# Block-sparse attention and a feed-forward net in one planned kernel: weight splits due later, late attention steps due later, one last eviction on VectorE

## The chip, the cores and the metric

The kernel runs on one NeuronCore of a Trainium2 chip. The metric is the device time of one execution in microseconds. Three executions of the kernel before took 785.02, 786.54 and 787.48 us; the median is 786.54 us.

## The reference

The inputs are `q`, `k` and `v` of shape (4, 8, 768, 64), three sampled key blocks for each of 24 query blocks, and two weight matrices `w_in` (512 x 2048) and `w_out` (2048 x 512), the weights and the samples in 64 bits.

```python
scores = scale * np.matmul(q, k.transpose(0, 1, 3, 2))
# a block of 32 queries sees: its own block and its neighbours, blocks 0 and 23, three sampled blocks;
# query blocks 0 and 23 see all keys
attn = softmax(np.where(mask, scores, -1e9))
x = (attn @ v).transpose(0, 2, 1, 3).reshape(3072, 512)
h = x @ w_in
out = (h - np.tanh(h)) @ w_out
```

## The kernel before

**Feed-forward units.** The 3072 tokens are cut into six chunks of 512 (`CHUNKS`, four query blocks of all four batches each), the 2048 hidden features into 16 tiles of 128. One pair of chunk and tile is a unit; there are 96 of them, numbered by `UNITS`. The first two chunks are worked off in halves: units 0 to 7 are the first half of chunk 0, 8 to 23 are chunk 1, 24 to 31 the second half of chunk 0, 32 to 47 chunk 2, and so on to 95. A unit has twelve matmuls of the first layer (`first`, four groups of three, as each operand is kept as a high and a low part), a bend of the hidden values by nine elementwise operations (`bent`), and twelve matmuls of the second layer (`second`, four groups of three, one for each 128 tokens), which come two and a half units later.

**Attention steps.** Attention for later chunks is worked off in steps beside the units. A step has 32 score products into banks 6 and 7 (`scores`), row maxima on VectorE (`most`), exponentials on ScalarE (`exps`), eight transposes on TensorE back into banks 6 and 7 (`turn`), two copies out of them (`copy`), 64 value products into bank 4 or 5 (`accum`), a normalisation on VectorE (`norm`), and a high and a low part written into the chunk's operand on ScalarE and GpSimd (`put`). Query blocks 0 and 23 see all keys; their steps come in threes (`EDGES`), have a single copy as their `norm`, and are joined afterwards by small VectorE operations (`weigh`, `join`). Ten early steps run before and around unit 0. `SLOTS` gives each later step its unit. In the tables for chunks 3, 4 and 5 (`m` of 3, 4, 5) a chunk of 16 units has eleven slots, at offsets 0, 1, 2, 4, 5, 7, 8, 10, 11, 13 and 14; ten of them are used in the last one. So 32 steps belong to these chunks.

**Order.** Nothing is scheduled freely. Each piece of work is put on a list with a due time in units (`at`), the list is sorted by due time, ties by the order of entry, and every engine keeps exactly that order (`InOrder`), SyncE's queue of transfers included. Due times of unit u: the four groups of `first` at u + 0, 0.125, 0.25, 0.375; the four groups of `second` for unit u - 2 at u + 0.5, 0.625, 0.75, 0.875; the nine operations of the bend by `STEPS`, of which `w`, `hs`, `t`, `qq`, `mk` and `gh` are ScalarE's, `p1`, `p2`, `p3` and `cp` VectorE's, `gl` GpSimd's and `th` GpSimd's up to unit 31 and VectorE's from 32 on. `cp`, due at u + 1.49, is the last that reads the hidden values' bank, 4 or 5 in turn. A step in slot s has its scores at s + 0.55, its row maxima at s + 0.63, its exponentials at s + 0.75 and 0.85, its transposes at s + 1.21 (where the next slot is the next unit) or s + 1.55, its copies 0.05 and 0.06 later, and its value products at 0.52 past the start of the next slot, 0.1 before the normalisation. The value products at u + 0.52 go to the bank of unit u - 1, so they need that unit's `cp` as well as the copies.

**Weights.** The 64-bit weights are turned into 32-bit ones on the chip, 32 tiles of 128 x 1024 words. `convert` is three VectorE operations, the first two through a spare PSUM bank. `split` writes the high part on ScalarE and the low part on GpSimd, `save` writes both to memory by SyncE for later units (`get`). Four tiles are converted before unit 0, the other 28 at the times in `CONVA` (twelve in units 0 to 7) and `CONVB` (every 0.93 units from 8.2 on). `split` is due 0.03 units after the third operation of its conversion, `save` 0.4 after it.

**The end.** `store` evicts the four accumulators of a chunk, j = 0 and 2 on ScalarE and j = 1 and 3 on VectorE, and sends each out in four transfers; for the last chunk those of j = 0 and 2 are issued by ScalarE's queue, those of j = 1 and 3 by SyncE's.

Of the kernel before, what the change touches and what calls it, by code (L numbers as in the profile page):

```python
# [11 lines left out]
F32 = mybir.dt.float32  # L12
# [5 lines left out]
ALU = mybir.AluOpType  # L18
# [4 lines left out]
P = 128  # L23
# [3 lines left out]
DM, DFF = 512, 2048  # L27
# [5 lines left out]
NU = NTOK // P // CT * NFT  # L33

LEAD, T0, RATE = 10, 10.25, 0.62
QUICK, TURN = 0.66, 1.0
NQ = 4
KEPT = 3
VW = H * (D + 1) // 2
# [27 lines left out]
class InOrder:  # L67


    class Engine:  # L70
        def __init__(self, tc, engine):
            self.tc, self.engine = tc, engine
# [44 lines left out]
class Unit:  # L117
# [27 lines left out]
    def at(self, half, j):  # L145

        return (half, self.b) if self.b else (self.f, (NB - 1) * half)


class Attention:  # L150
    def __init__(self, tc, k, q, v, samp, rows, ffn, ident, banks, att, sm, f2, rv, at):
        self.tc, self.nc = tc, InOrder(tc)
        self.k, self.q, self.v, self.ffn, self.ident, self.banks = k, q, v, ffn, ident, banks
        self.sm, self.f2, self.att, self.rv = sm, f2, att, rv
        self.ks = att.tile([P, 2, H, S], F32, name="ks")
        self.vws, self.krs, self.loans = {}, {}, {}
        ffn.lent = self.lent
        self.kx, self.vx = (att.tile([1, 66], I32, name=f"{n}x") for n in "kv")
        self.held = {}
        self.vals, self.qs, self.ve = {}, {}, {}  # L160
        self.ms, self.nbs, self.ps, self.pts, self.nbe, self.es, self.wts = ({} for _ in range(7))
        self.kept = [ffn.spare.bitcast(F32)[:, 256 * i : 256 * i + 256] for i in range(3)]

        units = []
        last = {}

        def add(c, time, **kw):
            u = Unit(len(units), c, time, **kw)
            u.i, u.before = c, last.get(c)
            if u.n < LEAD - 2:  # L170
                u.i, u.before = u.n % 2, units[u.n - 2] if u.n > 1 else None
            elif u.n < LEAD:
                u.before = units[u.n - 2]
            if u.b:
                last[c] = u
            units.append(u)

        for c in range(2):
            for b in CHUNKS[0]:
                add(c, 0, b=b)  # L180
        for c in range(2):
            add(c, 0, b=CHUNKS[1][0])
        for m, blocks in list(enumerate(CHUNKS))[1:]:
            steps = [(c, dict(b=b)) for b in blocks if 0 < b < NB - 1 for c in range(2)]
            edges = [(g // 2, dict(f=g % 2, k=k)) for g in EDGES.get(m, ()) for k in range(3)]
            steps += edges
            for i, (c, kw) in enumerate(steps[2 * (m == 1) :]):
                slots = SLOTS[m - 1]
                following = slots[i + 1] if i + 1 < len(slots) else 16 * m if m > 2 else slots[i] + 1
                add(c, slots[i] + 0.55, prod=following + 0.52, **kw)  # L190
        lead = lambda x: (x - T0) * RATE
        for u in units[:2]:
            at(lead(-9.05), self.load_q, u)
        for bt in range(2):
            at(lead(-9), self.load_k, 0, bt)
        at(lead(-9.1), self.load_samples, samp, rows)
        for bt in range(2):
            at(lead(-8.9), self.load_k, 1, bt)
        for u in units:
            t, n = u.t, u.n  # L200
            if u.b:
                if n > 1:
                    at(max(t["s"] - 2.0, units[n - NQ].t["s"] + 0.01) if n >= NQ else lead(-8.95 + 0.01 * n), self.load_q, u)
                at(max(t["s"] - 1.2, u.before.t["s"] + 0.01 if u.before else lead(-3)), self.gather_k, u)
                at(max(t["s"] - 2.0, u.before.t["pv"] + 0.01) if u.before else lead(-3 + 0.1 * n), self.gather_v, u)
            else:
                if u.k == 0:
                    at(units[n - 1].t["s"] + 0.02, self.load_q, u)
                at(units[n - 2].t["pv"] + 0.02, self.load_ve, u)
            at(t["s"], self.scores, u)  # L210
            at(t["m"], self.most, u)
            at(t["e1"], self.exps, u, 1)
            at(t["e0"], self.exps, u, 0)
            at(t["turn"], self.turn, u)
            at(t["c1"], self.copy, u, 1)
            at(t["c0"], self.copy, u, 0)
            at(t["pv"], self.accum, u)
            at(t["norm"], self.norm, u)
            if u.b:
                for x in "hl":  # L220
                    at(t["norm"] + (0.1 if x == "h" else 0.15), self.put, u, x)
            elif u.k == 2:
                at(t["e0"] + 0.12, self.weigh, u)
                end = 2 * u.c + u.f in EDGES[len(CHUNKS) - 1]
                quiet = iter([t["norm"] + 0.1 + 0.08 * j for j in range(6)] if end else self.quiet(units[u.n + 1 :], t["norm"]))
                for k in range(3):
                    for s in range(1 + k):
                        at(next(quiet), self.join, u, k, s)
                for i in range(2):
                    for x in "hl":  # L230
                        at(t["norm"] + 0.65 + 0.2 * i if end else LATE + 0.5 * (2 * u.c + u.f) + 0.25 * i, self.put, u, x, i)
# [250 lines left out]
class FFN:  # L482
# [134 lines left out]
    def store(self, n, j):  # L617
        nc = self.nc
        end = n == len(CHUNKS) - 1
        if n == 0:  # L620
            ob = self.work.pop(("sum", j))
            nc.vector.scalar_tensor_tensor(out=ob, in0=self.acc[j], scalar=-1.0, in1=ob, op0=ALU.mult, op1=ALU.add)
        elif j % 2:
            if n == 1:
                ob = self.spare.bitcast(F32)[:, DM * (j // 2) : DM * (j // 2) + DM]
            else:
                ob = self.f2.tile([P, DM], F32, tag="wcvt", name=f"ob{n}_{j}")
            nc.vector.tensor_scalar(out=ob, in0=self.acc[j], scalar1=-1.0, scalar2=None, op0=ALU.mult)
        else:
            ob = self.rv.tile([P, 1040], F32, tag="rv", name=f"ob{n}_{j}")[:, 0:DM]  # L630
            nc.scalar.activation(out=ob, in_=self.acc[j], func=AF.Copy, scale=-1.0)
        eng = nc.scalar if end and j % 2 == 0 else nc.sync
        for bt in range(B):
            r0 = S * bt + BLK * CHUNKS[n][j]
            eng.dma_start(out=self.out[r0 : r0 + BLK, :], in_=ob[BLK * bt : BLK * bt + BLK])

    def plan(self, at):
        t, done = lambda x: (x - T0) * RATE, []
# [3 lines left out]
        slots = [(t(4.5 + 1.6 * k), 0.3 * RATE, None) for k in range(4)] + [(x, 0.09, banks[b]) for x, b in zip(CONVA, CONVAB)]  # L642
        slots += [(CONVB[0] + CONVB[1] * k, 0.12, banks[6 + k % 2]) for k in range(2 * HALF)]
        free = []
        for k, ((m, ft), (t0, dt, tmp)) in enumerate(zip(halves[0] + halves[1], slots)):
            at(max(t0 - 1.8, free[k - 3] if k > 2 else -99), self.load, m, ft, k)
            for x in range(3):
                at(t0 + dt * x, self.convert, m, ft, x, tmp)
            end = t0 + 2 * dt
            at(end + 0.03 + 0.35 * (k == len(slots) - 1), self.split, m, ft)  # L650
            if ft >= KEPT:
                at(end + 0.4, self.save, m, ft)
            free.append(end + 0.01)
            done.append((m, UNITS.index((ft // HALF, ft))))
        self.ends = [e for e in ENDS if e != 2 * HALF]
        for u in range(NU):
            n, ft = UNITS[u]
# [10 lines left out]
            end = u == NU - 1  # L668
# [52 lines left out]
```

## Time and profile before

| what | value |
|---|---|
| median of three runs | 786.54 us |
| the profiled execution | 785.86 us, of which its span is 784.1 us |
| TensorE matmul busy | 728.9 us, 93% |
| VectorE busy | 549.9 us, 70% |
| ScalarE busy | 479.2 us, 61% |
| GpSimd busy | 337.2 us, 43% |
| mean granted TensorE clock | 0.98 |

The profile calls TensorE's matmuls PE and its weight loads PEld, VectorE DVE, ScalarE ACT, GpSimd POOL and SyncE SP; a trailing q is an engine's own queue of transfers. Names on the left of an arrow are what an instruction writes, on the right what it reads: `ps` is any PSUM bank, `vw,pt` and `ve,pt` the value products, `kr,q` and `ks,q` the scores, `ident,p` the transposes, `x,wi` (also `wri`, `li`) the first layer and `wo,gh` and `wo,gl` (also `wro`, `lo`) the second. `cvti` and `cvto` are converted tiles, `wi` and `wo` what a split writes. All instructions have one line, L78, that of a helper that records the order. "Busy" time of matmuls is modelled at its end, so start times are the firmer numbers.

### The profile page before, as it was taken

What the parts mean: (1) busy time and instruction counts of PE and PEld (TensorE: products, weight loads), DVE (VectorE), ACT (ScalarE), POOL (GpSimd) and SP (SyncE); (2) the same over time, 40 slices, a digit from 0 to 9 for tenths busy, and PEclk for the clock granted to TensorE, in tenths of its full rate; (3) what the DMA queues carried; (4) which work ended last, traced back from release to release, by engine and by line L of the source; (5) the groups of instructions that cost most, each with busy time, mean ns of one, the idle gap of its engine ahead of it and who ended that gap; (6) DMA issues with size and microseconds to landing.
All of it is one profiled execution on the core that took longest, in us unless ns stands there. A gap on an engine that the chain in (4) does not pass through costs nothing.

```text
span 784.1 us, 20699 instructions
## 1 busy us (share of the span) xinstructions
PE 728.9 (93%) x8128; PEld 564.7 (72%) x8128; DVE 549.9 (70%) x970; ACT 479.2 (61%) x1021; POOL 337.2 (43%) x406
## 2 busy tenths in 40 slices
PE   1777887999999999999999999999999998999996
PEld 0555555878777777777777777777877776788884
DVE  4566777779875765777676678676777675875653
ACT  1576756577767766565665666665666555554553
POOL 3685764667687646244322434321432211221211
PEclk9899999999999999999999999999999999999998
DMA  8887674489685686275746166565157364246542
GB/s 347 268 268 239 201 224 161 164 320 363 228 262 171 193 275 205 79 233 175 280 149 205 37 200 230 185 228 184 69 158 265 127 217 163 82 135 219 187 158 80
DMA packets 54260, 155.49 MB, mean 198 GB/s; under 512 B 9107, under 2 KB 15764, under 8 KB 53652
## 3 DMA queue, kind: packets, MB, share of 16 engines
q1 hardware_dynamic: 53780, 153.65, 58.6%
q8 instruction: 64, 1.05, 0.5%
q10 hardware_dynamic: 384, 0.52, 0.2%
q14 instruction: 32, 0.26, 0.1%
HBM read 133.17 MB, written 20.97 MB: 197 GB/s over the span
## 4 chain that ended last, share of the span: by engine, by line
PE 71%; DVE 7%; ACT 3%; issue 2%; POOL 1%; DMA 0%; DVEq 0%; POOLq 0%
PE ps L78 71%; DVE ps L78 3%; DVE t L78 1%; POOL gl L78 1%; DVE m L78 0%; ACT p L78 0%; ACT t L78 0%; DVE e L78 0%; ACT hs L78 0%; ACT wo L78 0%; ACT u L78 0%; DVE ob L78 0%; DVE cvti L78 0%; DVE cvto L78 0%; ACT gh L78 0%
## 5 line engine op out<-in xcount | busy, mean ns | idle before, releaser
L78 PE MATMUL ps<-x,wi 128*128 128x512 f32 x888 | 221.2, 393 | 0.0
L78 POOL TENSOR_TENSOR gl<-t,gh 128x512 fp32r<-128x512 f32 x96 | 124.3, 1295 | 215.3 <-ACT gh L78 69.5
L78 PE MATMUL ps<-wo,gh 128*128 128x512 f32 x592 | 192.2, 407 | 0.0
L78 PEld LDWEIGHTS ps<-x,wi 128*128 128x128 f32 x888 | 164.9, 188 | 35.5
L78 PEld LDWEIGHTS ps<-wo,gh 128*128 128x128 f32 x592 | 108.6, 190 | 36.9 <-issue 15.0
L78 ACT ACTIVATE u<-ps 128x512 f32<-128x512 f32 x96 | 57.3, 597 | 108.2 <-PE ps L78 108.2
L78 PE MATMUL ps<-wo,gl 128*128 128x512 f32 x296 | 117.6, 399 | 0.7 <-POOL gl L78 0.7
L78 POOL TENSOR_TENSOR x<-xt,x 128x256 fp32r<-128x256 f32 (+1 forms) x48 | 34.3, 715 | 161.8 <-ACT x L78 158.3
L78 POOL COPY kr<-ks 128x256 f32 (+2 forms) x188 | 98.5, 617 | 11.9 <-DMA ks<-k 11.7
L78 DVE TENSOR_REDUCE m<-ps 128x2 f32<-128x512 f32 x112 | 70.9, 673 | 19.1 <-PE ps L78 17.2
L78 DVE COPY_PREDICATED t<-mk,ps 128x512 f32<-128x512 int32 x96 | 71.8, 748 | 10.1 <-DVE ps L78 0.9
L78 DVE TENSOR_TENSOR ps<-ps,u 128x512 f32<-128x512 f32 x96 | 66.5, 692 | 13.7 <-ACT t L78 13.7
L78 ACT ACTIVATE p<-ps,nb 128x256 f32<-128x256 f32 x176 | 73.8, 471 | 2.9
L78 DVE SCALAR_TENSOR_TENSOR ps<-qq,ps 128x512 f32<-128x512 f32 x96 | 66.4, 692 | 12.9 <-ACT qq L78 8.6
L78 PEld LDWEIGHTS ps<-vw,pt 128*32 128x32 f32 x2816 | 44.4, 113 | 38.6 <-DVE t L78 10.1
L78 PE MATMUL ps<-vw,pt 128*32 128x65 f32 x2816 | 52.5, 227 | 20.4 <-DMA vw<-v 9.3
L78 ACT ACTIVATE qq<-u,bias 128x512 f32<-128x512 f32 x96 | 69.3, 722 | 0.0
L78 ACT ACTIVATE mk<-u,bias 128x512 f32<-128x512 f32 x96 | 69.1, 720 | 0.0
L78 DVE SCALAR_TENSOR_TENSOR ps<-u,ps 128x512 f32<-128x512 f32 x96 | 66.6, 693 | 2.5
L78 DVE TENSOR_TENSOR t<-t,ps 128x512 f32<-128x512 f32 x64 | 43.5, 680 | 35.2 <-ACT t L78 35.1
L78 PE MATMUL ps<-ident,p 128*128 128x128 f32 x448 | 62.4, 283 | 5.6 <-ACT p L78 4.2
L78 PEld LDWEIGHTS ps<-wo,gl 128*128 128x128 f32 x296 | 56.1, 189 | 15.4 <-POOL gl L78 1.9
(98 smaller groups left out, 980.2 us busy)
## 6 DMA issues: line engine op xcount, KB each, us to landing
wi<-w2i SPq DMA_DIRECT2D x65, 512.0 KB, 4.7
wo<-w2o SPq DMA_DIRECT2D x65, 512.0 KB, 3.7
vw<-v SPq DMA_DIRECT2D x186, 130.0 KB, 2.9
q<-q SPq DMA_DIRECT2D x52, 128.0 KB, 4.3
ve<-v SPq DMA_DIRECT2D x24, 260.0 KB, 4.0
ks<-k SPq DMA_DIRECT2D x4, 1536.0 KB, 8.4
rawo<-w SPq DMA_DIRECT2D x12, 512.0 KB, 4.3
rawi<-w SPq DMA_DIRECT2D x10, 512.0 KB, 4.7
```

What stands on the lines that cost most here:

```text
L78: r = f(*args, **kw)
```

## The change

Four due times and one engine change:

- Steps of chunks 3, 4 and 5 have every due time 0.08 units later. Their scores are due at s + 0.63, their value products at 0.60 past the next slot.
- `split` of the 28 tiles converted from unit 0 on is due 0.3 units after the conversion's third operation in place of 0.03; the last tile's stays at 0.38. `save` is due 0.65 after it in place of 0.4.
- For early steps 0 to 7, `put` is due 0.02 and 0.03 after `norm` in place of 0.1 and 0.15.
- In `store` of the last chunk, j = 2 is evicted by VectorE. Its transfers stay on ScalarE's queue.

```diff
-QUICK, TURN = 0.66, 1.0
+QUICK, TURN, SHIFT = 0.66, 1.0, 0.08
...
-                add(c, slots[i] + 0.55, prod=following + 0.52, **kw)
+                add(c, slots[i] + 0.55 + SHIFT * (m > 2), prod=following + 0.52 + SHIFT * (m > 2), **kw)
...
-                    at(t["norm"] + (0.1 if x == "h" else 0.15), self.put, u, x)
+                    at(t["norm"] + (0.1 if x == "h" else 0.15) * (0.2 if n < LEAD - 2 else 1), self.put, u, x)
...
+        elif end and j:
+            ob = self.rv.tile([P, 1040], F32, tag="rv", name=f"ob{n}_{j}")[:, 0:DM]
+            nc.vector.tensor_scalar(out=ob, in0=self.acc[j], scalar1=-1.0, scalar2=None, op0=ALU.mult)
         else:
...
-            at(end + 0.03 + 0.35 * (k == len(slots) - 1), self.split, m, ft)
+            at(end + (0.03 if t0 < 0 else 0.38 if k == len(slots) - 1 else 0.3), self.split, m, ft)
             if ft >= KEPT:
-                at(end + 0.4, self.save, m, ft)
+                at(end + 0.65, self.save, m, ft)
```

## Rows read from the trace of the kernel before

**Rows 1.** Busy time by stretch: us, then busy us (instructions) of each engine, clock, DMA

```profile
core 0: us, PE busy (x) PEld busy (x) DVE busy (x) ACT busy (x) POOL busy (x), PEclk, DMA share, GB/s
62.00:142.00 80.00, 64.80 (x912) 47.24 (x911) 57.58 (x110) 54.00 (x120) 48.24 (x57) 0.91 0.63 201
142.00:680.00 538.00, 531.97 (x5905) 415.39 (x5904) 393.57 (x684) 343.33 (x729) 227.47 (x268) 1.00 0.58 196
```

**Rows 2.** TensorE's waits, whole span: total us, times, longest us

```profile
PE ps L78 <- ACT wo L78: 7.3, 4, 2.1
...
PE ps L78 <- DVE t L78: 4.3, 5, 2.2
```

**Rows 3.** Timeline of all engines, unit 5: start, duration, what, [idle before, releaser]

```profile
125.74 0.72 DVE L78 COPY_PREDICATED t<-mk,ps 128x512 f32<-128x512 int32 x1
125.85 0.63 ACT L78 ACTIVATE wo<-cvto 128x512 fp32r<-128x512 f32 x1 [2.28 <-DVE cvto L78]
...
126.56 0.26 PE L78 MATMUL ps<-vw,pt 128*32 128x65 f32 x4 [1.64 <-ACT wo L78]
```

**Rows 4.** Timeline of TensorE, one group of the second layer ahead of transposes

```profile
406.37 0.63 PE L78 MATMUL ps<-wo,gh 128*128 128x512 f32 x2
...
407.07 1.03 PE L78 MATMUL ps<-ident,p 128*128 128x128 f32 x8
```

**Rows 5.** Timeline of TensorE in unit 65, a step's products between second-layer groups

```profile
568.05 0.63 PE L78 MATMUL ps<-wo,gh 128*128 128x512 f32 x2
...
568.84 1.11 PE L78 MATMUL ps<-vw,pt 128*32 128x65 f32 x64
569.88 1.09 PE L78 MATMUL ps<-kr,q 64*32 64x256 f32 x32
570.91 0.73 PE L78 MATMUL ps<-wo,gh 128*128 128x512 f32 x2
...
573.11 1.08 PE L78 MATMUL ps<-x,wri 128*128 128x512 f32 x4
```

**Rows 6.** Timeline of TensorE in unit 78, value products with no scores behind

```profile
673.52 1.11 PE L78 MATMUL ps<-ve,pt 128*32 128x65 f32 x64
674.57 0.73 PE L78 MATMUL ps<-wo,gh 128*128 128x512 f32 x2
...
676.77 1.08 PE L78 MATMUL ps<-x,wi 128*128 128x512 f32 x4
```

**Rows 7.** Timeline of VectorE around the products of rows 5

```profile
566.50 0.69 DVE L78 COPY pt<-ps 128x512 f32<-128x512 f32 x1 [0.88 <-PE ps L78]
...
567.90 0.74 DVE L78 COPY_PREDICATED t<-mk,ps 128x512 f32<-128x512 int32 x1
...
571.26 1.25 DVE L78 TENSOR_REDUCE m<-ps 128x2 f32<-128x512 f32 x2
```

**Rows 8.** Timeline of VectorE in unit 74: the row maxima

```profile
640.25 1.29 DVE L78 TENSOR_REDUCE m<-ps 128x2 f32<-128x512 f32 x2 [0.64 <-PE ps L78]
```

**Rows 9.** Timeline of VectorE in unit 78: the end of unit 77's bend

```profile
672.72 0.75 DVE L78 COPY_PREDICATED t<-mk,ps 128x512 f32<-128x512 int32 x1
```

**Rows 10.** Timeline of all engines, unit 1

```profile
77.21 0.63 ACT L78 ACTIVATE wro<-cvto 128x512 fp32r<-128x512 f32 x1 [1.51 <-DVE cvto L78]
...
79.47 0.66 PE L78 MATMUL ps<-ident,p 128*128 128x128 f32 x4 [2.45 <-ACT p L78]
...
80.89 0.73 DVE L78 COPY_PREDICATED t<-mk,ps 128x512 f32<-128x512 int32 x1
...
82.44 0.66 PE L78 MATMUL ps<-vw,pt 128*32 128x65 f32 x16
```

**Rows 11.** Timeline of all engines, unit 0: last early step and first layer

```profile
63.20 0.45 DVE L78 STREAM_TRANSPOSE xt<-x 128x256 f32<-128x256 f32 x1
...
66.28 0.57 PE L78 MATMUL ps<-x,wri 128*128 128x512 f32 x1 [2.08 <-ACT x L78]
```

**Rows 12.** Timeline of the end: transfers of the last chunk by two queues

```profile
777.38 3.63 SPq L78 DMA_DIRECT2D out<-ob  x8
...
779.61 1.85 ACTq L78 DMA_DIRECT2D out<-ob  x4
```

## The prediction

> **What bounds the kernel now.** I read the busy times by stretch first, then TensorE's waits, then the timelines where a due time moves past another. From 142 to 680 us TensorE's matmuls are busy 532.0 of 538 us at the full clock [rows 1]: there TensorE's own order is the time, and nothing done elsewhere can give back more than 6 us. From 62 to 142 us it is busy 64.8 of 80 us, with a mean granted clock of 0.91, so some 14 us of these ran at the lower level, 1.2 GHz [rows 1]. Here the other engines set the time.
>
> The list of waits names the splits of output weights as the largest releaser in this stretch: four waits, 7.3 us [rows 2], and one part of the change moves exactly these. I don't take the name at its word. In one of the four, the predicated copy that ends a unit's bend runs 125.74 to 126.46 and the split 125.85 to 126.48; the value products start at 126.56 [rows 3]. Both end within 0.02 us, and by the code the products read nothing that the split writes, but they overwrite the bank that the predicated copy has just read. Both follow the same conversion. So the true releaser is VectorE, whose list in these units (two conversions, the bend, the row maxima, the normalisation) is the loop; ScalarE's split is beside it.
>
> **The shift by 0.08, on TensorE.** The second-layer groups of a unit are due at 0.5, 0.625, 0.75 and 0.875. Before, value products (0.52) and scores (0.55) lay together between the first two. After, value products (0.60) still lie there, but scores (0.63) come behind the second group by 0.005. The order group, values, scores, three groups becomes group, values, group, scores, two groups: one return to the second layer and one departure more. What these cost: a group of three with transposes behind takes 407.07 - 406.37 = 0.70 us [rows 4]. With value products behind it takes 568.84 - 568.05 = 0.79 [rows 5]. A departure costs 0.09. Three groups behind scores take 573.11 - 570.91 = 2.20 [rows 5], behind value products alone 676.77 - 674.57 = 2.20 [rows 6], against 3 x 0.70 = 2.10. A return costs 0.10, from either kind. Going straight from values to scores adds nothing that is saved now: the 64 products take 1.04 us with scores behind (569.88 - 568.84) and 1.05 with a group behind (674.57 - 673.52) [rows 5, 6].
>
> So 0.19 us for each slot where values and scores meet: 32 slots less the first, which has no values of an earlier step that moves with it, is 31. 31 x 0.19 = 5.9 us. No idle time covers it: all such stretches show TensorE with no gap but five waits of 4.3 us in total [rows 2]. The transposes (1.21 to 1.29, or 1.55 to 1.63) pass one group as well, but stand between two groups of the same layer before and after: no switch more.
>
> What the departure from values to scores would cost is in no row for scores; taken as for values. The bounds: nothing, if the scores' weights load under the group in between (0.10 x 31 = 3.1 us in all), and twice that of values (0.28 x 31 = 8.7).
>
> A rule of the Trainium skill speaks against this term. TensorE: Matmul & The Clock Gate, section "Step-by-step: what each phase is for", says that TensorE pulls weight loads ahead of matmuls in flight, so that the next tile's weights load while this one runs. By that, a change of shape would cost nothing and the term would be 0. The trace does not agree: 0.09 and 0.10 us stand at each such switch.
>
> **The shift, on VectorE.** Scores end 0.89 us later after the value products (0.70 + 0.10 + 0.09), and the row maxima wait for them. In a usual step this fits. In unit 65 the copy out of the transposes waited 0.88 us with the bend's third product queued behind it, and the predicated copy ended at 568.64, ready for the value products at 568.84 [rows 5, 7]. After, the copy (due 0.34) stands behind that product (0.27), which fills the gap: copy at 566.50 + 0.89 = 567.39, 0.7 for it and 0.74 for the predicated copy makes 568.83, against 568.84 + 0.19 = 569.03 on TensorE. The row maxima of steps with the full normalisation start at 571.26, 0.35 us behind the scores' end at 570.91 [rows 5, 7]; they lose less than 0.89.
>
> Two places have no such gap. In unit 74 five joins follow the maxima, VectorE is full to the predicated copy, and the value products already wait 2.2 us [rows 2]. The maxima there wait for the scores alone (0.64 idle, [rows 8]), so all 0.89 goes through: 0.89 - 0.19 = 0.7 more. In unit 77 the weights of the joins lie in the chain; its predicated copy ends 673.47 and the products start 673.52 [rows 6, 9]: again 0.7. Where a chunk's accumulators are evicted (due in units 33, 49 and 65) an eviction or a join moves into the time in which VectorE waits for the value products, which about pays for the later maxima. Of the 2.1 us of other waits [rows 2] 0.2 may be taken up. Together 5.9 + 0.7 + 0.7 - 0.2 = 7.1 us more. ScalarE's order (the high part of the bend ahead of the exponentials) and GpSimd's (low parts and key gathers 0.08 later) have room in these units.
>
> **The splits.** In units 3 to 6 VectorE is the loop, and ScalarE's list between the row maxima and the two copies stays as long: the input split that stood ahead of the copies goes behind them, while the output split, now due at 0.77, comes in between the two exponentials. I take nothing; the bounds are 7.3 us back, if the profile's releaser were the true one, and 2 us lost, if the exponentials' delay reaches the transposes. In unit 1 ScalarE is the bound: it idles 1.51 us for a conversion ahead of a split, with half a step's exponentials queued behind, and the second transposes wait 2.45 us [rows 10]. After, the split is due at 1.23, behind them, and the transposes can go up to 1.51 + 0.63 = 2.1 us earlier. But the value products then wait for the predicated copy, which ends at 81.62 where they start at 82.44 [rows 10]: 0.8 us. With a little for the other early units: 1.0. In units 8 to 31 TensorE is full and the splits are off its path; 0.5 of the 6 us of idle time up to 680 us [rows 1], as ScalarE's first squares of a unit no longer stand behind a split. GpSimd's low parts and the saves on SyncE come later too: the value gathers for a step, due at 0.53, now go out ahead of an input tile's save (0.69 in place of 0.44), and no get of a saved tile is nearer than five units.
>
> **The early puts.** The last early step's tile is transposed at 63.65, but ScalarE writes its part only after two sets of exponentials and copies, and the first layer waits 2.08 us for it [rows 11]. After, the put stands ahead of them. But for all eight early steps ScalarE then stops for the normalisation, with the next steps' exponentials and copies behind it, and the early steps follow each other more strictly. I take 0.5 us gained, between 2.1 gained and 2 lost.
>
> **The end.** ScalarE's eviction of the third quarter stood behind its own first four transfers; its last transfer was issued at 779.61 + 1.85 = 781.46, SyncE's at 777.38 + 3.63 = 781.01 [rows 12]. After, VectorE has the tile ready early, ScalarE's queue ends before SyncE's, and SyncE's is last: 0.45 gained. SyncE's own order is unchanged.
>
> **Sum.** 7.1 - 1.0 - 0.5 - 0.5 - 0.45 = 4.65 us. The profiled execution took 785.86 us (span 784.1), so 790.5; it lies 0.7 below the median of 786.54, which gives 791.2. I say 791.0.
>
> **Rivals.** *The profile's releaser is right* (14%): the four waits of 7.3 us are the splits' own and go. 791.0 - 7.3 = 783.7, and 784 to 786 if VectorE holds the products for part of it. Not slower. For it: the name in the list. Against: the code and the common end. It decides once more than 4.65 us come back.
>
> *The switch hides* (9%): the scores' order costs TensorE nothing, and only VectorE's 1.2 us stay. 791.0 - 5.9 = 785.1. This is where the skill's rule above would lead. Against: every switch in rows 5 and 6.
>
> *The later maxima hold every close pair* (10%): 17 pairs of steps lie in adjacent units; 13 beside those named. If swapping the copy and the product returns nothing, each loses up to 0.5: 791.0 + 6.5 = 797.5. Against: the 0.88 us gap.
>
> *The early part gets longer* (9%): ScalarE stopped by puts, and key gathers on GpSimd behind the later low parts, so that scores in units 4 and 5 come late. 2 us each: 795.
>
> *My forecast* (58%): own range 788 to 794, as the lower clock in the early units may fall on other places; a stretch of it costs up to half its length.
>
> **The numbers.** What a measurement of this kernel can tell from no change is about 0.3%, 2.4 us: 784.2 to 788.9. The forecast falls below 788.9 in one case of seven. Slower: 0.49 + 0.10 + 0.09 = 0.68. The first two rivals split: 0.11 faster; the rest, 0.21, within. The range reaches to the middle of the rivals on both sides: 785.0 to 796.0.
>
> **What would show it.** The second group between values and scores, 0.89 us in all, in the 31 slots; the wait in unit 74 near 3 us; a small one in 78. The waits called after the output split should stay near 7 us under another name, the predicated copy's. The transposes' wait in unit 1 should fall below 0.6. The last transfer should be SyncE's. Wrong would be an interval of the 31 slots unchanged, or value products in units 3 to 6 with no wait.

## The result, and the profile after

The changed kernel takes 792.07 us (median of 8 runs, 788.82 to 793.63), the kernel before 785.78 us (median of 8, 782.52 to 787.48): a ratio of 1.0078, 95% interval 1.0060 to 1.0096. It is 6 us slower. The prediction was 791.0. The profiled execution took 792.95 us (span 790.5), 7.1 us more than the one before.

Where the 7.1 us arise is read from the timelines: the start of each unit's first matmul, the changed kernel against the one before. (Worked out from the timelines of TensorE in both profiles; us.)

```
unit                      0      1      3      8     32     48     64     81     95    end
later than before     +2.14  -1.29  +0.19  -0.55  -1.08  +1.01  +3.56  +5.93  +5.93  +6.4
```

Up to unit 32 the changed kernel is 1.1 us ahead; from there to unit 81 it loses 7.0; the end costs 0.5 (span 790.5 - 784.1 = 6.4), and 0.7 lie outside the span.

The loss shows best in unit 65, where TensorE's timeline (start, duration, what) answers to [rows 5]:

```profile
572.62 1.11 PE L78 MATMUL ps<-vw,pt 128*32 128x65 f32 x64
573.66 0.73 PE L78 MATMUL ps<-wo,gh 128*128 128x512 f32 x2
...
574.56 1.09 PE L78 MATMUL ps<-kr,q 64*32 64x256 f32 x32
575.58 0.73 PE L78 MATMUL ps<-wo,gh 128*128 128x512 f32 x2
```

The second group stands between value products and scores and takes 574.56 - 573.66 = 0.90 us, where a group in mid-run takes 0.70. In a usual slot the unit is 0.20 or 0.21 us longer than before.

The two stretches of [rows 1] (us, then busy us (instructions) of each engine, granted clock, DMA):

```profile
62.00:142.00 80.00, 64.36 (x983) 46.94 (x984) 59.35 (x112) 55.02 (x125) 47.28 (x56) 0.98 0.61 189
142.00:680.00 538.00, 531.39 (x5859) 406.92 (x5862) 383.89 (x672) 343.19 (x727) 226.16 (x268) 1.00 0.60 196
```

TensorE is as full from 142 to 680 us as before; the loss is busy time, not idle time.

TensorE's waits, answering to [rows 2] (total us, times, longest):

```profile
PE ps L78 <- ACT pt L78: 7.2, 5, 1.8
PE ps L78 <- ACT t L78: 7.2, 4, 2.3
```

The releaser "ACT wo" is gone from the list, and the time isn't: the value products of units 3 to 6 still wait, 7.1 us in all (three of the four under "ACT t", whose fourth is unit 1's 2.34, and 2.22 in unit 6 for which no releaser is named). In unit 5, all engines, answering to [rows 3]:

```profile
124.39 0.60 ACT L78 ACTIVATE t<-ps 128x512 f32<-128x512 f32 x1
...
124.90 0.71 DVE L78 COPY_PREDICATED t<-mk,ps 128x512 f32<-128x512 int32 x1
...
125.72 1.14 PE L78 MATMUL ps<-vw,pt 128*32 128x65 f32 x64 [1.63 <-ACT t L78]
```

The wait was 1.64 and is 1.63. The products start 0.11 us after the predicated copy's end (125.61), 0.73 after that of the ScalarE operation now named (124.99).

Unit 1, TensorE, answering to [rows 10]:

```profile
76.03 0.66 PE L78 MATMUL ps<-ident,p 128*128 128x128 f32 x4 [0.30 <-ACT p L78]
...
80.42 1.66 PE L78 MATMUL ps<-vw,pt 128*32 128x65 f32 x64 [2.34 <-ACT t L78]
```

The transposes' wait fell from 2.45 to 0.30, and came back as 2.34 at the value products.

VectorE in unit 74, answering to [rows 8]:

```profile
646.39 1.29 DVE L78 TENSOR_REDUCE m<-ps 128x2 f32<-128x512 f32 x2 [1.53 <-PE ps L78]
...
652.56 0.67 DVE L78 SCALAR_TENSOR_TENSOR ps<-qq,ps 128x512 f32<-128x512 f32 x1
653.14 0.67 DVE L78 COPY pt<-ps 128x512 f32<-128x512 f32 x1
653.74 0.71 DVE L78 COPY_PREDICATED t<-mk,ps 128x512 f32<-128x512 int32 x1
```

The maxima wait 0.89 longer for the scores (1.53 against 0.64), and VectorE is full from there to the predicated copy. The value products behind it wait 2.29 us, 2.22 before.

The end, all engines, answering to [rows 12]:

```profile
781.91 1.09 PE L78 MATMUL ps<-wo,gl 128*128 128x512 f32 x4
...
782.58 1.88 DVE L78 TENSOR_SCALAR ob<-ps 128x512 f32<-128x512 f32 x3 [3.35 <-PE ps L78]
782.97 4.41 ACTq L78 DMA_DIRECT2D out<-ob  x8
783.30 4.12 SPq L78 DMA_DIRECT2D out<-ob  x8
```

SyncE's transfer is the last to be issued, at 787.42, ScalarE's at 787.38. Each of ScalarE's eight took 4.41/8 = 0.55 us, where four took 1.85 before (0.46).

### The profile page after: what moved, and what is told of

Same layout as the page of the kernel before. It is cut to its first block, busy times and chain, and to the rows that moved or that the text cites. A ratio compares the mean times of both kernels' runs of the same rounds, so it can differ in the third digit from the quotient of the medians.

```text
span 790.5 us, 20689 instructions
## 1 busy us (share of the span) xinstructions
PE 730.9 (92%) x8128; PEld 558.2 (71%) x8128; DVE 546.2 (69%) x971; ACT 479.5 (61%) x1020; POOL 336.2 (43%) x406
## 4 chain that ended last, share of the span: by engine, by line
PE 74%; DVE 4%; POOL 2%; issue 2%; ACT 1%; DMA 1%; DVEq 0%; POOLq 0%; ACTq 0%
PE ps L78 74%; DVE ps L78 2%; POOL gl L78 1%; DVE t L78 1%; POOL t L78 1%; DMA vw<-v 1%; DVE m L78 1%; POOL li L78 0%; DVE ob L78 0%; DVE sums L78 0%; DVE e L78 0%; ACT p L78 0%; POOL wo L78 0%; ACT hs L78 0%; ACT t L78 0%
## 5 line engine op out<-in xcount | busy, mean ns | idle before, releaser
L78 PEld LDWEIGHTS ps<-wo,gh 128*128 128x128 f32 x592 | 105.6, 188 | 36.3 <-issue 14.6
L78 DVE TENSOR_TENSOR ps<-ps,u 128x512 f32<-128x512 f32 x96 | 66.5, 693 | 11.6 <-ACT t L78 11.5
L78 ACT ACTIVATE x<-xt 128x256 fp32r<-128x256 f32 (+1 forms) x48 | 19.6, 408 | 86.5 <-DVE xt L78 86.5
L78 PE MATMUL ps<-kr,q 64*32 64x256 f32 x1408 | 52.0, 403 | 16.2 <-POOL kr L78 15.8
```

Source lines behind the costliest of these rows:

```text
L78: r = f(*args, **kw)
```

## The experiments

All times are medians beside runs of the kernel before in the same comparison (785.5 to 786.4 us). The order of the list is that of the questions.

**The shift alone.**

```diff
-QUICK, TURN = 0.66, 1.0
+QUICK, TURN, SHIFT = 0.66, 1.0, 0.08
...
-                add(c, slots[i] + 0.55, prod=following + 0.52, **kw)
+                add(c, slots[i] + 0.55 + SHIFT * (m > 2), prod=following + 0.52 + SHIFT * (m > 2), **kw)
```

> The kernel before with the shift of 0.08 alone. My theory (a second-layer group now stands between value products and scores, 0.19 us in each slot): starts of units up to 32 as before within 0.3 us, then some 0.19 to 0.20 more per slot with both products, unit 81 7.0 us later than unit 32 against before; time 7.0 us above before, about 792.8 on the scale of 785.8. Rival A, that the loss of the changed kernel comes from its early part and its end and the shift only adds part of it: 2 to 4 us above before. Rival B, that the shift costs nothing on TensorE: within 1.2 us of before.

Measured: 792.61 against 785.53, ratio 1.0097 (1.0079 to 1.0116). Unit 81 came 4.19 + 2.85 = 7.04 us later against unit 32 than before. The shift makes the whole loss, and of the expected size. Its early part is the code of the kernel before, and yet unit 32 started 2.85 us sooner in this trace: single executions differ by that much before unit 32, so that early edits have to be judged by their medians.

**The shift at 0.07**, against the last kernel.

```diff
-QUICK, TURN, SHIFT = 0.66, 1.0, 0.08
+QUICK, TURN, SHIFT = 0.66, 1.0, 0.07
```

> The kernel before with a shift of 0.07 in place of 0.08: scores are then due at 0.62, just ahead of the second group at 0.625, and value products, scores stay together; the due times of the bend, the row maxima, the exponentials, the copies and GpSimd's work against the steps move almost as with 0.08. My theory: the interval between two units in a slot stays as before, unit 81 against unit 32 within 0.7 us of before, time within 1 us of before. Rival, that the loss comes from the order on VectorE, ScalarE or GpSimd (later maxima, the copy behind the third product of the bend): 4 to 7 us above before, growing slot by slot as with 0.08.

Measured: 782.98 us, ratio 0.9972 (0.9951 to 0.9992): not equal but faster, and 9.6 us below the same kernel with 0.08. Unit 81 against unit 32: 3.45 us sooner than before. TensorE in unit 65:

```profile
564.74 1.11 PE L78 MATMUL ps<-vw,pt 128*32 128x65 f32 x64
565.78 1.09 PE L78 MATMUL ps<-kr,q 64*32 64x256 f32 x32
566.81 0.73 PE L78 MATMUL ps<-wo,gh 128*128 128x512 f32 x2
```

The two products are together. The gain lies in four places, the waits at value products where VectorE is full: units 34 (0.59), 50 (0.36), 66 (0.36) and 75 (2.18). For the last, all engines behind unit 74's maxima, first in the kernel before:

```profile
642.70 1.29 POOL L78 TENSOR_TENSOR gl<-t,gh 128x512 fp32r<-128x512 f32 x1 [7.11 <-ACT nbe L78]
...
643.33 0.95 DVE L78 TENSOR_TENSOR e<-e,e 128x260 f32<-128x260 f32 x1
...
648.98 1.11 PE L78 MATMUL ps<-ve,pt 128*32 128x65 f32 x64 [2.22 <-DVE t L78]
```

and in this run:

```profile
638.98 0.43 DVE L78 TENSOR_TENSOR e<-e,e 128x260 f32<-128x260 f32 x1
...
641.97 0.67 DVE L78 SCALAR_TENSOR_TENSOR ps<-qq,ps 128x512 f32<-128x512 f32 x1
...
642.54 0.68 DVE L78 COPY pt<-ps 128x512 f32<-128x512 f32 x1
...
643.14 0.72 DVE L78 COPY_PREDICATED t<-mk,ps 128x512 f32<-128x512 int32 x1
...
643.92 0.78 PE L78 MATMUL ps<-ve,pt 128*32 128x65 f32 x40 [1.62 <-DVE t L78]
```

The value products wait 1.62 us in place of 2.22. The greater part of this, 0.42, is in VectorE's five joins: one of them took 0.95 us beside GpSimd's low part of the hidden values and takes 0.43 here. With any shift ScalarE's high part (due 0.78) goes ahead of the exponentials (0.75 before, 0.82 here), so GpSimd's low part starts 4.7 us into unit 74 in place of 8.2, long before the joins. The other 0.2 is the order at the end: the bend's third product now stands ahead of the copy, and the predicated copy no longer comes straight behind the product whose result it reads. In units 34, 50 and 66 that exchange gives nothing; there an eviction (0.60) or a join (0.37) has moved out of the stretch in which VectorE is full. All this is read from the traces; no run makes one of these moves alone. At 0.08 the same moves were made in unit 74, and the later maxima took them back: 1.62 + 0.89 - 0.19 = 2.32; measured 2.29.

The other 1.6 of the 2.18 us are the clock. Behind the wait of 2.22 us the kernel before was granted the lower level, 1.2 GHz, for some 3 us; the two windows in which that shows (the last numbers of a row are granted clock, DMA share, GB/s):

```profile
650.00:652.00 2.00, 2.00 (x41) 0.93 (x34) 0.51 (x2) 0.00 (x0) 0.00 (x0) 0.56 0.38 98
652.00:654.00 2.00, 2.00 (x6) 1.57 (x7) 2.00 (x4) 1.32 (x4) 0.00 (x0) 0.59 0.83 225
```

The changed kernel with a shift of 0 (below) waited just as long there and kept 2.4 GHz, as this kernel did behind 1.62:

```profile
650.00:652.00 2.00, 2.00 (x89) 1.37 (x78) 0.53 (x2) 0.00 (x0) 0.00 (x0) 1.00 0.09 21
652.00:654.00 2.00, 2.00 (x10) 1.59 (x10) 2.00 (x4) 1.34 (x4) 0.00 (x0) 1.00 0.66 189
```

That unit took 12.56 us before and 10.98 with the clock kept.

**The shift at 0.11**, against the same: both products later, but together.

```diff
-QUICK, TURN, SHIFT = 0.66, 1.0, 0.08
+QUICK, TURN, SHIFT = 0.66, 1.0, 0.11
```

> The kernel before with a shift of 0.11: value products due at 0.63 and scores at 0.66, both behind the second group at 0.625 and ahead of the third at 0.75. They lie together again, and both are 0.70 us later than before. My theory (the loss at 0.08 is the second-layer group between the two, by 0.19 us of TensorE for each slot and by row maxima that come 0.9 us late against the rest): neither is here, so unit 81 against unit 32 stands as with 0.07, 1.8 to 3.5 us earlier than before, and the time is 1 to 4 us below before. Rival, that being later in the unit is what costs: slower than before, 5 us or more, as with 0.08.

Measured: 784.25 us, ratio 0.9976 (0.9958 to 0.9993). Unit 81 against unit 32: 2.38 us sooner than before (expected at least 1.8). TensorE in unit 65:

```profile
571.02 1.11 PE L78 MATMUL ps<-vw,pt 128*32 128x65 f32 x64
572.06 1.09 PE L78 MATMUL ps<-kr,q 64*32 64x256 f32 x32
573.09 0.73 PE L78 MATMUL ps<-wo,gh 128*128 128x512 f32 x2
```

So it is not lateness that costs. Of the three shifts only 0.08 parts the two products.

**Scores alone later by 0.08.**

```diff
-            at(t["s"], self.scores, u)
+            at(t["s"] + 0.08 * (n >= 24), self.scores, u)
```

> The kernel before with the scores alone 0.08 later for the 32 steps of chunks 3 to 5; every other due time of a step (row maxima, exponentials, transposes, copies, value products) as before. My theory: TensorE's switch alone makes the loss, 31 slots of 0.19 = 5.9 us, and with it the places where VectorE is full; unit 81 against unit 32 6 to 8 us later than before, time 6 to 8 us above before. Rival, that the loss needs the moved order of the other engines: below 2 us.

Measured: 804.26 us, ratio 1.0236 (1.0205 to 1.0267), 18.7 us above before where at most 8 were expected; unit 81 against unit 32 20.0 us later. Of the usual units, those whose predecessor has no slot lost 0.18 to 0.20 us, the switch alone; those whose predecessor has one lost 0.45 to 0.47. The 0.25 on top is in the eight transposes, here in unit 72:

```profile
630.77 1.28 PE L78 MATMUL ps<-ident,p 128*128 128x128 f32 x8
```

and in unit 65 of the changed kernel:

```profile
570.26 1.03 PE L78 MATMUL ps<-ident,p 128*128 128x128 f32 x8
```

The maxima come later, with them the exponentials, and the second four transposes wait for these (0.30 us from the start of the fourth to that of the fifth, in place of 0.11). That is my third rival's loss, later maxima that hold the close pairs, but by ScalarE's exponentials and not by VectorE's copy. In the changed kernel the transposes stand three matmuls of the first layer later, and only those of units 50 and 66 are held, by 0.15 us each.

And in unit 72 the scores waited for their queries, with the lower clock behind it (the profile's timeline, and a window of the same trace):

```profile
639.79 1.96 PE L78 MATMUL ps<-ks,q 64*32 64x256 f32 x32 [3.71 <-DMA q<-q]
```

```profile
640.00:642.00 2.00, 2.00 (x33) 0.79 (x22) 0.14 (x1) 0.00 (x0) 0.00 (x0) 0.50 0.80 289
```

That unit lost 6.3 us, and by the code this is the edit's own doing. The kernel keeps query tiles by name; the load for the steps of slots 74 to 77, due at 72.57, replaces the tiles that the scores of slot 72 read. In the kernel before these scores stand ahead of it and read the older tiles; moved to 72.63 they stand behind it and wait for the new transfer (issued at 636.10), which in the kernel before nothing reads until slot 74. This part of the loss says nothing about the switch.

**All but the shift**: the changed kernel with

```diff
-QUICK, TURN, SHIFT = 0.66, 1.0, 0.08
+QUICK, TURN, SHIFT = 0.66, 1.0, 0.0
```

> The changed kernel with the shift set to 0: later splits and saves, early puts and the last half's third quarter on VectorE stay. My theory: the early part gives 1.1 us back up to unit 32, from there to unit 95 nothing differs from before, and the end costs 0.5 us: 0.6 us below before, within 0.3% of it. Rival A, that these three edits carry part of the loss: 1 to 3 us above before. Rival B, that they are a gain which the shift hides: 2 to 3 us below before.

Measured: 783.08 us, ratio 0.9968 (0.9950 to 0.9985): 2.5 us below before, as rival B said and my theory from the trace did not. The three edits together gain.

**The puts alone.**

```diff
-                    at(t["norm"] + (0.1 if x == "h" else 0.15), self.put, u, x)
+                    at(t["norm"] + (0.1 if x == "h" else 0.15) * (0.2 if n < LEAD - 2 else 1), self.put, u, x)
```

> The kernel before with the early puts alone. Theory A, as the changed kernel's trace suggests: ScalarE stops for the normalisations of the early steps, unit 0 starts 2 to 3 us later, and the first layer's waits for the last early step's tile add little back: 0.5 to 2 us above before. Theory B, my prediction's: the put ahead of two sets of exponentials brings unit 0's third wait forward, 0.5 us below before, with unit 1 some 2 us earlier against unit 0.

Measured: 782.83 us against 785.53, ratio 0.9958 (0.9936 to 0.9981). Theory A is wrong in sign, theory B in size. Unit 0, TensorE, answering to [rows 11]:

```profile
64.65 3.39 PE L78 MATMUL ps<-x,wri 128*128 128x512 f32 x12
```

The first layer runs through. Unit 0 took 7.72 to 7.73 us in all seven traces with early puts, and 8.9 to 12.0 (mean 10.7) in the seven without. Unit 0 itself starts later, 65.6 against 63.9 in the mean of the same traces, so 1.3 us are left; the rest of the median's 2.7 the traces don't locate. The granted clock of all executions points to it: 0.988 in the mean with early puts, 0.984 before. As an estimate from these, twice the missing share of the span, each execution spends some 5.6 us less at the lower level; how much of that TensorE would have waited anyway isn't known.

**The splits alone.**

```diff
-            at(end + 0.03 + 0.35 * (k == len(slots) - 1), self.split, m, ft)
+            at(end + (0.03 if t0 < 0 else 0.38 if k == len(slots) - 1 else 0.3), self.split, m, ft)
             if ft >= KEPT:
-                at(end + 0.4, self.save, m, ft)
+                at(end + 0.65, self.save, m, ft)
```

> The kernel before with the later splits and saves alone. My theory: in unit 1 the transposes' wait of 2.45 us goes below 0.6; units 3 to 6 keep waits of about 7 us in all at the value products, under another name (VectorE's loop is the bound there); 0.5 us back between units 8 and 32; nothing in the late units. Time 1 to 2.5 us below before. Rival A, the profile's releaser is right: the waits at the value products of units 3 to 6 go and the time is 5 to 7 us below before. Rival B, that the splits gain nothing and the gain of the three edits comes from the puts: within 0.7 us of before, and unit 1 unchanged.

Measured: 785.21 us, ratio 1.0001 (0.9981 to 1.0020): nothing gained, which is rival B's time. Units 8 to 32 gave the 0.5 us (0.48). TensorE in units 1 and 2:

```profile
79.95 0.66 PE L78 MATMUL ps<-ident,p 128*128 128x128 f32 x4 [0.31 <-ACT p L78]
...
84.36 1.20 PE L78 MATMUL ps<-vw,pt 128*32 128x65 f32 x64 [2.35 <-ACT t L78]
...
93.89 0.50 PE L78 MATMUL ps<-wro,gl 128*128 128x512 f32 x1 [1.23 <-POOL gl L78]
```

Unit 1 took 10.15 us, 1.2 less than in the profile of the kernel before, but not by the splits: in three traces whose early part is the code of the kernel before (scores alone, third quarter alone, shift of 0.11) it took 10.1 to 10.2 too. In all fourteen traces it is 10.1 to 10.2 where no lower clock was granted in it and 11.3 to 11.5 where one was, whatever the splits. With the shift of 0.11, splits as before, all engines in unit 1:

```profile
82.12 0.66 PE L78 MATMUL ps<-ident,p 128*128 128x128 f32 x4 [2.45 <-ACT p L78]
...
83.54 0.74 DVE L78 COPY_PREDICATED t<-mk,ps 128x512 f32<-128x512 int32 x1
...
84.38 1.14 PE L78 MATMUL ps<-vw,pt 128*32 128x65 f32 x64 [0.21 <-issue]
```

The transposes wait their 2.45 us, and yet the value products start 0.10 us behind the predicated copy's end (84.28), 8.0 us into the unit, as with late splits. So the predicated copy bounds unit 1 either way, and the 0.8 us between it and the products in [rows 10] were TensorE at the lower clock (0.55 and 0.59 granted in the windows from 80 to 82 and 82 to 84 us of that trace).

Unit 2 became 1.4 us longer: GpSimd does the low part of a late split just ahead of the activations' low part, which the second layer waits for. It takes 12.0 to 12.1 us in the four traces with all splits late and 10.6 to 10.8 in the ten others. I had put that GpSimd work down as harmless.

**The third quarter alone.**

```diff
+        elif end and j:
+            ob = self.rv.tile([P, 1040], F32, tag="rv", name=f"ob{n}_{j}")[:, 0:DM]
+            nc.vector.tensor_scalar(out=ob, in0=self.acc[j], scalar1=-1.0, scalar2=None, op0=ALU.mult)
```

> The kernel before with only the eviction of the last half's third quarter on VectorE. My prediction: ScalarE's queue ends early, SyncE's ends last as before, 0.45 us less behind the last matmul. Rival, from the changed kernel's trace: both queues issue their eight transfers at the same time and each issue takes 0.5 to 0.55 us in place of 0.45, so the last one is issued later against the last matmul, 0.4 to 0.5 us more behind it.

Measured, in one profile (784.9 us). The two queues:

```profile
776.16 3.86 ACTq L78 DMA_DIRECT2D out<-ob  x8
776.48 3.84 SPq L78 DMA_DIRECT2D out<-ob  x8
```

From the start of the last low-part matmuls (775.09) to the end of the span (783.1) it is 8.0 us; before 784.1 - 776.00 = 8.1, in the changed kernel 790.5 - 781.91 = 8.6. Over all traces it is 8.19 in the mean of the six with this edit and 8.20 in the eight without. Neither forecast holds: the issues take 0.48 us each in three of the six and 0.51 to 0.57 in the others, against 0.45 to 0.47 before. The edit is worth nothing.

**The changed kernel with 0.07**:

```diff
-QUICK, TURN, SHIFT = 0.66, 1.0, 0.08
+QUICK, TURN, SHIFT = 0.66, 1.0, 0.07
```

> The changed kernel with a shift of 0.07 in place of 0.08, all else as in it. My theory: the loss of the changed kernel is the place of the scores behind the second group, 0.01 units; with them ahead of it the late units gain as they did with 0.07 alone (2.2 us by the median), the early puts give their part, and the time is 4 to 5 us below before, 10 us below the changed kernel. Rival, that later splits or the end interact with the shift: more than 2 us above that.

Measured: 782.61 us against 786.43, ratio 0.9951 (0.9932 to 0.9969): a hundredth of a unit turns 6 us lost into 4 gained.

**The shift at 0.07 with the early puts; and that with late splits from unit 8 on and the third quarter on VectorE.** The first is the two edits above on the kernel before; the second adds the third quarter's and

```diff
-            at(end + 0.03 + 0.35 * (k == len(slots) - 1), self.split, m, ft)
+            at(end + (0.03 if t0 < 8 else 0.38 if k == len(slots) - 1 else 0.3), self.split, m, ft)
             if ft >= KEPT:
-                at(end + 0.4, self.save, m, ft)
+                at(end + (0.4 if t0 < 8 else 0.65), self.save, m, ft)
```

> The kernel before with the shift of 0.07 and the early puts; splits, saves and the end as before. My theory: 2.2 us from the shift and some 3 from the puts, 4 to 6 us below before; the splits of the changed kernel give nothing, so this stands within 1 us of the version that has them. Rival, that the two gains overlap (both are fewer stretches at the lower clock): only 2.5 us below before.

> As the last one, and with splits and saves late only for conversions from unit 8 on, and the third quarter's eviction on VectorE. My theory: 0.5 us less between units 8 and 32 and 0.1 less at the end, no wait of 1.2 us for GpSimd's low part of the activations in unit 2; 0.6 us below the last one, which the times alone can't show, so read from the starts of units. Rival: no difference in the starts of units 8 to 32.

Measured: 779.90 us, ratio 0.9918 (0.9888 to 0.9947), and 779.17 us, ratio 0.9907 (0.9877 to 0.9936). Both beat both kernels; between the two the times can't tell, and units 8 to 32 took 0.27 us less in the second. Both beat the version with all splits late, by 2.7 and 3.4 us of the medians: I had expected at most 1. The waits of TensorE from 62 to 150 us, first with all splits late, then with those of units 0 to 7 as before:

```profile
PE ps L78 <- ACT t L78: 7.2, 4, 2.3
...
PE ps L78 <- ACT p L78: 1.9, 4, 0.8
...
PE ps L78 <- POOL gl L78: 1.2, 1, 1.2
```

```profile
PE ps L78 <- ACT wo L78: 7.1, 4, 2.1
PE ps L78 <- ACT p L78: 4.0, 4, 2.5
```

The transposes' wait (under "ACT p") is 2.1 us shorter with late splits; 2.3 at unit 1's value products (under "ACT t") and 1.2 for GpSimd come in its place.

**The same pair without the shift.** This is the kernel with all but the shift, and

```diff
-            at(end + (0.03 if t0 < 0 else 0.38 if k == len(slots) - 1 else 0.3), self.split, m, ft)
+            at(end + (0.03 if t0 < 8 else 0.38 if k == len(slots) - 1 else 0.3), self.split, m, ft)
             if ft >= KEPT:
-                at(end + 0.65, self.save, m, ft)
+                at(end + (0.4 if t0 < 8 else 0.65), self.save, m, ft)
```

> The changed kernel with the shift at 0 and with splits and saves late only from unit 8 on; puts early, third quarter on VectorE. The same pair with the shift at 0.07 differed by 3 us, in favour of early splits as before; with the shift at 0 the version with all splits late stood only 0.4 us above the one with none. Theory A, the late splits of units 0 to 7 cost some 3 us whenever the puts are early (a wait of 1.2 us for GpSimd in unit 2, longer waits at the value products and more time at the lower clock behind them): 5 to 6 us below before, 3 us below the version with all splits late. Theory B, they cost next to nothing: 2 to 3.5 us below before. In either case the wait for GpSimd's low part in unit 2 should be gone and unit 2 1.3 us shorter.

Measured: 781.52 us, ratio 0.9947 (0.9929 to 0.9965), 1.6 us below the version with all splits late, between the two theories. The wait for GpSimd is gone, and unit 2 took 10.7 us (12.05 there). Beside early puts the late splits of units 0 to 7 cost 2.7 and 3.4 us with the shift at 0.07, and here 1.6, which alone would not be clear of the noise; without early puts they cost nothing measurable. Unit 2 holds 1.4 of it. It isn't the clock: the mean granted clock of all executions is 0.989 or 0.990 in each of these five versions. Where the rest arises stays open.

## Why the prediction came out

The sum was 1.1 us below the measured median, but it is right by its largest term alone; three of the small ones had the wrong sign or size.

- **The shift, 7.1 us: right in sum (7.0), half right in parts.** A second-layer group between the products costs 0.20 or 0.21 us in each of 27 usual slots, as forecast. The Trainium skill (TensorE: Matmul & The Clock Gate, "Step-by-step: what each phase is for") says that the next tile's weights load while this one's matmul runs. By that the group would cost nothing; the trace doesn't agree, at 0.2 us for each slot. The late transposes, put at nothing, cost 0.03 us in most of the units between the slots, 0.4 in all. The two places on VectorE are wrong: I charged 0.7 us each, and the value products wait 0.07 longer behind unit 74 (2.29 against 2.22) and not at all behind unit 77; the wait near 3 us and the small one in unit 78 that I named as signs didn't come. The move of ScalarE's high part that I had said there was room for frees VectorE from GpSimd's operation in both places: the join of 0.95 us takes 0.43, and the weights of 1.13 us (last section) take 0.17. In units 34, 50 and 66 the eviction or join pays for the later maxima, as I had said (waits of 1.13 against 1.19, and 0.39 against 0.37 twice), but in units 50 and 66 the transposes are held for 0.15. What I didn't see is that these moves are a gain where the maxima aren't late: 3.5 us at 0.07, 1.6 of them the clock. Against a shift of 0.07 the place of the scores costs 10.5 us, 5.9 in usual slots and the units between them and 4.6 in the four with a wait.
- **The releaser that the profile names: right.** The split left, the wait stayed (1.64 and 1.63 us in unit 5), under another name.
- **The splits, -1.5 us: wrong.** Units 8 to 31 gave the 0.5. In unit 1 the transposes' wait fell as forecast, but the value products then wait for the predicated copy as long: the 0.8 us that I read as room behind it was TensorE at the lower clock in that one execution. Unit 2 pays 1.4 us on GpSimd. Alone the edit is worth 0.0 (-1.5 to +1.6).
- **The puts, -0.5 us: mis-sized**, -2.7 measured (-5.0 to -1.5). The last early step's tile is ready for unit 0 in every run, and the 2.08 us go entirely.
- **The end, -0.45 us: wrong.** The sum kept 0.45 us for each issue; with both queues issuing eight in a row they take 0.48 to 0.57, and the end is as long as before (8.19 against 8.20).

That 791.0 lies so near to 792.1 is in part luck. The three small edits were to give 2.45 us and with the shift at 0 they gave 2.5, but the puts gave it and not the splits or the end. With the shift they gave less: the change cost 6.3 us in the comparison where I had said 4.5 (791.0 against 786.54), 1.7 more than the shift alone and the three without it add up to (7.1 - 2.5); the intervals allow that, and no run explains it. And the three executions that I started from had a median 0.8 above that of the eight in the comparison, which brought the two times closer.

## What to carry to other kernels

Where an engine keeps a sorted order, a moved due time is judged by what it crosses, not by how far it moves: 0.07, 0.08 and 0.11 gave 2.5 us gained, 7.1 lost and 1.3 gained. List every pair that changes places on every engine, price each change of kind on a full engine from rows where it already happens, and look for the same move one step short of a crossing. Rows of one execution can hold a stretch at the lower clock: a gap read there is checked in a second one. And where a test moves one piece of work alone, see what it reads once it has passed its neighbours. A name behind a wait is checked against what the waiting instruction reads and overwrites before anything is built on it.

## What the hardware showed beside this

A VectorE operation on 12 numbers took 1.13 us in the kernel before, and was in the chain that I called tight in unit 77. All engines, before:

```profile
669.49 1.29 POOL L78 TENSOR_TENSOR gl<-t,gh 128x512 fp32r<-128x512 f32 x1 [7.11 <-ACT nbe L78]
669.68 1.13 DVE L78 TENSOR_TENSOR w<-mn,nbe 128x12 f32<-128x12 f32 x1
```

and VectorE after:

```profile
676.26 0.17 DVE L78 TENSOR_TENSOR w<-mn,nbe 128x12 f32<-128x12 f32 x1
```

It ended with GpSimd's operation (670.81 and 670.78). There are four such operations in a trace. In all fourteen traces they took 1.11 to 1.13 us in the seven in which GpSimd's operation had begun 0.19 or 0.20 us ahead (no shift, or the scores alone), and 0.17 in the seven with a shift, where GpSimd does it elsewhere. The Trainium skill (SBUF — State Buffer, "Who interferes with whom") says that a VectorE instruction with two inputs in SBUF contends with a GpSimd instruction that reads SBUF, and that issue order decides which of the two blocks. The traces agree: in the seven with the long operation VectorE's is the second. I had taken the row's 1.13 us for the operation's own price.

The lower clock behind a wait of 2.2 us is not certain: of the eight traces with this wait in unit 75 six show it, and two don't (the shift at 0, and the splits alone), though the engines' orders there are those of the kernel before. Such a stretch is worth 1.6 us, as much as most of the edits here.
